# Two short terms in one product, later placement of one weight row, and 128 rows in every rounded product: a change to the opening of a one-core kernel

## The chip, the cores and the metric

One core of a Trainium2 chip runs the whole program. The metric is device time in microseconds (us) of that core. The kernel before took 1107.01 us, the median of three runs (1104.09 to 1109.41). PE is the matrix engine, PEld its weight load, DVE, ACT and POOL the vector, scalar and GpSimd engines, and SP the engine whose queue issues nearly all the DMAs.

## The reference

The reference takes `x` of 2 x 3008 x 256 float32 and does three things in a row:

```
X   = fft(fft(x, axis=1), axis=2).real           # 2 x 3008 x 256, then 6016 tokens x 256
h   = X @ w_in;   g = max(h, 0)**2;   Y = g @ w_out          # 256 -> 2048 -> 256
h   = Y @ w2_in;  P = a0 + a1*h + a2*h**2 + a3*h**3
Q   = 1 + |b0|*|h| + |b1|*h**2;   out = (P / (Q + 1e-6)) @ w2_out
```

The four weight matrices arrive as float64. The kernel turns each into a float32 on the chip and splits it into a rounded high part and a low part (`hi`, `lo`), so that a product is made of three fast products in the rounded type f32r. A product in plain f32 is made of two passes of the matrix engine, and shows as two PE instructions.

## The kernel before, in words

The Fourier transform over 3008 = 64 x 47 points is a product with 47-point tables (the "U phase"), a product along the 256 features (`f_d`, lines 488 and 489), and a 64-point product (`f_s`, lines 511 to 518). The 64 residues fold to 31 pairs of rows and two single ones. The two single ones are the first terms `x0` (line 251); the 31 others come in chunks of four rows (`X_CH`, chunks 1 to 7), then two, then one. A row has 188 terms for each feature: 128 in one slice, 60 in another. The host lays two rows beside one another as three slices of 128 partitions: 128 terms of the first row, 128 terms of the second, and a slice that holds the 60 left of the first (partitions 0 to 59) and the 60 left of the second (64 to 123). The table `c47` has zeros where the other row's terms lie. So line 255 multiplies the 128 terms and line 256 the 60 left, both for each row by itself, and for each half of the 256 features. ACT copies one half out of PSUM (line 265), and DVE adds and subtracts the two (line 272) into `U`.

Beside that, the 16 chunks W0 to W15 of the first weight matrices are loaded (lines 328 and 330) and prepared: an absolute value on ACT (335), a clamp, two bit operations and two merges on DVE (338 to 352), a sum and a difference (359), rounding on ACT (367) and the low part on DVE (372). Row 128 of `w_in` belongs to a feature of its own. It is loaded (377), prepared (381 to 395), placed by three small DMAs on rows 0, 32 and 64 of a zeroed tile `w0` of 65 rows (400), and rounded (404). Its product with `X0` is line 624 for the first two tiles of tokens and line 643 for the other ten. `X0` comes from a product with the same weight column repeated 65 times (lines 513 and 518).

The tokens go in one tile of 384 columns and eleven of 512. Each tile passes the first layer (`h1`, lines 623 to 643, and `o1`, line 669), and then the second (`h2`, line 610, and `o2`, line 669) in halves of 256 columns. Where a half's `o2` begins, one product of a row of zeros with a row of weights (line 660) clears a whole bank of PSUM.

A planner (`Queues`) sets the order: each operation has an engine, a cost in us, a place and buffers that it takes and gives, and the planner writes the operations out in the order in which its own clock starts them. An engine then runs its instructions in that order. `HOT0` and `HOT` put products on a tile of zeros (`hot_t`, line 281) ahead of and between the chunks of the U phase; `SPILL_W` says after which weight chunk `U` is written to memory for the later tiles (line 320).

Of the kernel before, what the change touches and what calls it, by code (L numbers as in the profile page):

```python
# [47 lines left out]
U_SPLIT, U_REST = 0, -7.32  # L48
HOT0, HOT = 8, (2, 11, 6, 2, 0, 0, 0, 0, 0)
DMA_LAT = 2.41  # L50
C_AT, S_AT, S_STEP = -21.12, -5.27, 3
W_AT = (-4.0, 20.0)
AB_AT = -40
W_TAGS = (("g2", "x2h", "g2", "x2l"), ("g2",))
W2_AT, W2_STEP = 6.94, 1.11
W_FIRST, SPILL_W = (0, 0, 1, 1, 2, 2, 3, 3, 4, 4), 12

# [100 lines left out]
def body(ctx: ExitStack, tc: tile.TileContext, x0, xf, w1i, w1o, w2i, w2o, a_in, b_in,  # L158
# [15 lines left out]
    ab = const.tile([128, 6], F32, name="ab")  # L174
    w0f = const.tile([65, NF, 128], F32, name="w0")
    w0 = w0f.bitcast(F32R)
    zero = const.tile([1, 128], F32R, name="zero")
    a0, a1, a2, b0 = (ab[:, i:i + 1] for i in (0, 1, 2, 4))
# [55 lines left out]
    def x_load(c):  # L234
        XT[c] = stp.tile([128, 6, 256], F32, tag="xt", name="xt", bufs=SLOTS["xt"])
        if c == 0:
            nc.sync.dma_start(out=XT[c][0:96, 0:4].rearrange("p (s h) d -> p s h d", h=2), in_=x0)
            return
        p = (S0[c] - 1) // 2
        for k in range((XN[c] + 1) // 2):  # L240
            o, a = XT[c][:, 3 * k:3 * k + 3], xf[p + k]
            if 2 * k + 2 > XN[c]:
                o, a = o[:, 0:3:2], a[:, 0:3:2]
            nc.sync.dma_start(out=o, in_=a)

    def u_mm(c, dc, tag):
        PU[c, dc] = p = ps(tag, [128, 4, 128])
        d = slice(dc * 128, (dc + 1) * 128)
        if c == 0:
            for i in range(4):  # L250
                nc.tensor.matmul(p[:, 0, 0:96], XT[c][0:96, i, d], c47_t[0:96, 3 + i], start=(i == 0), stop=(i == 3))
        else:
            for i in range(XN[c]):
                k, h = 3 * (i // 2), i % 2
                nc.tensor.matmul(p[:, i, 0:94], XT[c][:, k + h, d], c47_t[:, 0, 0:94], start=True, stop=False)
                nc.tensor.matmul(p[:, i, 0:94], XT[c][:, k + 2, d], c47_t[:, 1 + h, 0:94], start=False, stop=True)

# [27 lines left out]
    for c in range(NC):  # L285
        place = -32 + c
        n = XN[c]
        add(("x", c), "SP", 0.54 * n if c else 7.0, place, lambda c=c: x_load(c), take=("xt",), lat=X_LAT,
            after=[("wd", W_FIRST[c] - 1)] if W_FIRST[c] else [])
# [5 lines left out]
        for dc in range(2):  # L295
            add(("um", c, dc), "PE", (2 * n if c else 4) * mm4(96), place, lambda c=c, dc=dc, g=tags[dc]: u_mm(c, dc, g),
                needs=[("x", c)] + ([("hot", c)] if c and HOT[c - 1] and not dc else []), take=(tags[dc],), give=("xt",) if dc else (), lat=0.2)
# [104 lines left out]
    def w0_round():  # L402
        nc.scalar.activation(out=zero, in_=hot_t[0:1], func=ACTF.Copy)
        nc.scalar.activation(out=w0, in_=w0f, func=ACTF.Copy)
# [4 lines left out]
    add("w0p", "DVE", 1.6, -31, w0_parts, needs=["w0a"], give=("g2",), port=True)  # L409
    add("w0c", "SP", 2.4, -31, w0_place, needs=["w0p", "w0z"], give=("cw",), lat=2.5)  # L410
    add("w0", "ACT", act(2048), -20, w0_round, needs=["w0c"])
# [94 lines left out]
    def f_s(t, k, tag):  # L506
        v = FU.pop((t, k, "v"))
        f = ps(tag, [128, 512])
        FU[t, k] = p, r = f[:, 0:256].rearrange("p (c n) -> p c n", c=2), f[0:65, 256:384]
        if t + k == 0:  # L510
            nc.tensor.matmul(p[:, 0, :], v[:, 0:128], r0c, start=True, stop=True)
            nc.tensor.matmul(p[:, 1, :], v[:, 129:257], r0s, start=True, stop=True)
            nc.tensor.matmul(r, v[:, 128:129].to_broadcast([66, 65]), r0c, start=True, stop=True)
        else:
            for u in range(2):
                cols = slice(u * 64, u * 64 + 64)
                nc.tensor.matmul(p[:, :, cols], v[:, u, 0:128], rcs[:, u], start=True, stop=True)
                nc.tensor.matmul(r[:, cols], v[:, u, 128:129].to_broadcast([128, 65]), rcs[:, u, 0], start=True, stop=True)


    def f_eh(t, k, i):
        if i == 0:
            X1[t] = [sb("x1" + part, [128, 2, NMAX // 2], F32R) for part in "hl"]
            X0[t] = sb("x0", [65, NMAX // 2], F32R)
        cols = slice(i * 128, i * 128 + 128)
        p, r = FU[t, k]
        nc.scalar.activation(out=X1[t][0][:, :, cols], in_=p, func=ACTF.Copy)
        nc.scalar.activation(out=X0[t][:, cols], in_=r, func=ACTF.Copy)
# [123 lines left out]
    def mm_o(G, W, O, tag, t, j, first, gs):  # L652
        n = NW[t] if tag == "o1" else SUB[t][2]
        one = tag == "o2" and t > 0
        if j == 0:
            if one:
                o = ps("o2a", [128, NMAX])[:, :2 * n]
                O[t], OB[t] = [o[:, :n], o[:, n:]], o

                nc.tensor.matmul(o, zero, W["hi"][0][0:1, :2 * n], start=True, stop=False)  # L660
            else:
                O[t] = [ps((o1_tag(t) if tag == "o1" else tag) + part, [128, NMAX])[:, :n] for part in "ab"]
# [356 lines left out]
```

## Time and profile before

| | |
|---|---|
| Median of three runs | 1107.01 us |
| The profiled execution | 1106.53 us, its span 1104.8 us |
| PE busy | 1069.3 us, 7790 instructions |
| DVE busy | 1012.6 us |
| ACT busy | 985.7 us |
| POOL busy | 489.9 us |
| Mean granted clock of PE | 0.995 |

The span runs from the first to the last instruction; 1.7 us of the execution lie around it. A row of the timeline gives the start, the length, the engine and line, and the tiles written and read; matmuls overlap, so that the cost of one in a stream is the distance from its start to the next one's, not its length. A form such as `65*128 65x256` is 65 rows by 128 columns of weights, and 256 columns that pass through them.

### The profile page before, as it was taken

The numbers are of one execution on the slowest core, as the hardware profiler recorded it, in microseconds if no ns is written. First come the engines' busy times: TensorE is split into PE (matmuls) and PEld (weight loads), VectorE is DVE, ScalarE is ACT, GpSimd is POOL, SyncE is SP. The second block draws the span as 40 slices with busy tenths as digits, with TensorE's granted clock in tenths as the row PEclk, the third lists the DMA queues.
The fourth block names the chain that finished last, engine by engine and source line by source line (L and its number), as shares of the span: only waits on it lengthen the run. The fifth ranks groups of instructions, "written<-read, shape, count | busy, mean of one in ns | idle before, by whom it ended". The sixth has DMA issues, their size and how long they took to land.

```text
span 1104.8 us, 21504 instructions
## 1 busy us (share of the span) xinstructions
PE 1069.3 (97%) x7790; PEld 1003.3 (91%) x7790; DVE 1012.6 (92%) x1806; ACT 985.7 (89%) x2009; POOL 489.9 (44%) x373
## 2 busy tenths in 40 slices
PE   7999988999999999999999999999999999999986
PEld 7989987899999999989999999999998999999985
DVE  2799999999999999999998999999899999889997
ACT  2488887999998989899999999999999999999896
POOL 0000003545545555455545545545544555545476
PEclk9999989999999999999999999999999999999999
DMA  6753410000000000000000000000000000000000
GB/s 228 259 207 99 160 39 1 2 25 11 1 20 11 1 20 11 1 20 11 1 12 18 1 11 20 2 11 20 1 20 11 2 10 11 1 10 11 1 11 20
DMA packets 26838, 36.83 MB, mean 33 GB/s; under 512 B 2315, under 2 KB 19341, under 8 KB 26733
## 3 DMA queue, kind: packets, MB, share of 16 engines
q1 hardware_dynamic: 26589, 35.33, 9.6%
q8 instruction: 62, 1.02, 0.4%
q14 instruction: 43, 0.35, 0.1%
q10 hardware_dynamic: 144, 0.13, 0.0%
HBM read 26.65 MB, written 8.78 MB: 32 GB/s over the span
## 4 chain that ended last, share of the span: by engine, by line
PE 61%; DVE 17%; ACT 16%; issue 4%; DMA 1%; POOL 1%; SPq 0%; DVEq 0%; POOLq 0%; ACTq 0%
PE o2a L669 15%; PE p L610 12%; PE o1a L669 7%; PE o1b L669 7%; PE p L641 5%; PE o2b L610 3%; DVE g L775 2%; PE o2b L641 2%; ACT y L758 2%; DVE p L781 2%; ACT t L735 2%; ACT y L762 2%; DVE t L749 2%; ACT u L745 2%; DVE t L753 1%
## 5 line engine op out<-in xcount | busy, mean ns | idle before, releaser
L792 POOL TENSOR_TENSOR g<-t,y 128x512 fp32r<-128x512 f32 (+1 forms) x182 | 247.1, 1358 | 406.9 <-DVE t L788 312.5
L712 POOL TENSOR_TENSOR g<-g,g 128x512 fp32r<-128x512 f32 x160 | 213.1, 1332 | 189.9 <-ACT g L707 131.9
L669 PE MATMUL o2a<-g,w2hi 128*128 128x256 f32 (+1 forms) x1440 | 263.0, 283 | 5.8 <-POOL g L792 5.5
L669 PEld LDWEIGHTS o2a<-g,w2hi 128*128 128x128 f32 x1440 | 209.1, 189 | 16.6 <-POOL g L792 7.8
L775 DVE SCALAR_TENSOR_TENSOR g<-t,ab,y 128x512 fp32r<-128x512 f32 (+1 forms) x177 | 140.9, 798 | 11.1 <-ACT y L762 8.3
L669 PE MATMUL o2a<-g,w2lo 128*128 128x256 f32 (+1 forms) x720 | 144.4, 280 | 0.0
L669 PE MATMUL o1a<-g,w1hi 128*128 128x512 f32 x352 | 139.7, 397 | 1.5 <-DVE g L712 1.0
L669 PE MATMUL o1b<-g,w1hi 128*128 128x512 f32 x352 | 138.9, 395 | 0.0
L781 DVE SCALAR_TENSOR_TENSOR p<-u,g 128x512 f32<-128x512 f32 (+2 forms) x178 | 132.1, 742 | 0.7
L788 DVE SCALAR_TENSOR_TENSOR t<-t,ab,p 128x512 f32<-128x512 f32 (+2 forms) x178 | 129.0, 724 | 1.2
L741 DVE SCALAR_TENSOR_TENSOR u<-u,ab,p 128x512 f32<-128x512 f32 (+1 forms) x141 | 102.1, 724 | 26.6 <-ACT t L735 25.7
L745 ACT ACTIVATE u<-u 128x512 f32<-128x512 f32 (+2 forms) x178 | 110.0, 619 | 13.8 <-DVE u L741 13.4
L610 PE MATMUL p<-x2h,w2hi 128*128 128x256 f32 (+1 forms) x558 | 114.8, 287 | 6.6 <-DVE t L753 2.3
L762 ACT ACTIVATE y<-y 128x512 f32<-128x512 f32 (+1 forms) x185 | 115.0, 623 | 1.4
L758 ACT ACTIVATE y<-u 128x512 f32<-128x512 f32 (+1 forms) x177 | 109.3, 618 | 5.0 <-POOL g L792 2.5
L610 PE MATMUL p<-x2l,w2hi 128*128 128x256 f32 (+1 forms) x558 | 113.0, 284 | 0.0
L610 PE MATMUL p<-x2h,w2lo 128*128 128x256 f32 (+1 forms) x558 | 112.9, 284 | 0.0
L697 ACT ACTIVATE g<-g 128x512 f32<-128x512 f32 x160 | 100.7, 630 | 11.8 <-DVE g L687 11.2
L703 ACT ACTIVATE g<-g 128x512 fp32r<-128x512 f32 (+1 forms) x175 | 109.4, 625 | 2.0 <-PE o1b L669 0.5
L669 PEld LDWEIGHTS o2a<-g,w2lo 128*128 128x128 f32 x720 | 110.3, 188 | 0.0
L707 ACT ACTIVATE g<-g 128x512 f32<-128x512 f32 (+1 forms) x175 | 109.0, 624 | 1.0
L753 DVE SCALAR_TENSOR_TENSOR t<-t,ab,p 128x512 f32<-128x512 f32 (+1 forms) x143 | 103.0, 721 | 0.5
(272 smaller groups left out, 2886.8 us busy)
## 6 DMA issues: line engine op xcount, KB each, us to landing
g<-in_dram SPq DMA_DIRECT2D x48, 256.0 KB, 3.2
xt<-in_dram SPq DMA_DIRECT2D x16, 384.0 KB, 7.0
out_dram<-os SPq DMA_DIRECT2D x21, 256.0 KB, 2.1
udram<-U SPq DMA_DIRECT2D x4, 640.0 KB, 5.6
ut<-udram SPq DMA_DIRECT2D x10, 256.0 KB, 3.0
x2h<-in_dram SPq DMA_DIRECT2D x8, 256.0 KB, 5.7
x2l<-in_dram SPq DMA_DIRECT2D x8, 256.0 KB, 5.1
out_dram<-os SPq DMA_DIRECT2D x2, 192.0 KB, 1.9
```

What stands on the lines that cost most here:

```text
L610: nc.tensor.matmul(h[:, c * n:(c + 1) * n], l[:, k, :], r[:, k], start=(q == 0), stop=(q == 5))
L669: nc.tensor.matmul(O[t][e], l[:, e * 128:(e + 1) * 128], r[:, c * n:(c + 1) * n], start=(i == 0 and q == 0 and not one), stop=(i == NF - 1 ...
L703: nc.scalar.activation(out=e["gh"], in_=e["g"], func=ACTF.Square)
L712: eng.tensor_tensor(out=e["gl"], in0=e["g"], in1=f32(e["gh"]), op=ALU.subtract)
L745: nc.scalar.activation(out=w, in_=w, func=ACTF.Abs)
L753: nc.vector.scalar_tensor_tensor(out=t1, in0=t1, scalar=a1, in1=H2[t, j], op0=ALU.add, op1=ALU.mult)
L758: nc.scalar.activation(out=e["z"], in_=e["w"], func=ACTF.Abs_reciprocal_sqrt, bias=Q1)
L762: nc.scalar.activation(out=z, in_=z, func=ACTF.Square)
L775: nc.vector.scalar_tensor_tensor(out=e["gh"], in0=e["t1"], scalar=a0, in1=e["z"], op0=ALU.add, op1=ALU.mult)
L781: nc.vector.scalar_tensor_tensor(out=e["m"], in0=e["w"], scalar=Q1, in1=f32(e["gh"]), op0=ALU.add, op1=ALU.mult)
L788: nc.vector.scalar_tensor_tensor(out=e["t1"], in0=e["t1"], scalar=a0, in1=e["m"], op0=ALU.add, op1=ALU.subtract)
L792: nc.gpsimd.tensor_tensor(out=e["gl"], in0=e["t1"], in1=e["z"], op=ALU.mult)
```

## The change

The two rows' terms that are left (60 each) go through one product of 188 columns for both rows, the 128 terms of each row follow as before, and line 256 is gone. The first terms `x0` are issued by ACT's queue, ahead of its first instruction. The small tables `a` and `b` go from the head of SP's queue to a place behind weight chunk W7. The three placing DMAs of row 128 wait until chunk 6 of `x` is issued. The products on zeros between the chunks go (21 of them), and the first group has ten in place of eight. `U` is written out after W16 in place of W12. `w0`, `X0` and the zeros have 128 rows in place of 65 and 1, and so the weight column of lines 513 and 518 is repeated 128 times.

```diff
-HOT0, HOT = 8, (2, 11, 6, 2, 0, 0, 0, 0, 0)
+HOT0, HOT, W0_AFTER = 10, (0, 0, 0, 0, 0, 0, 0, 0, 0), 6
-AB_AT = -40
+AB_AT = 0
-W_FIRST, SPILL_W = (0, 0, 1, 1, 2, 2, 3, 3, 4, 4), 12
+W_FIRST, SPILL_W = (0, 0, 1, 1, 2, 2, 3, 3, 4, 4), 16
-    w0f = const.tile([65, NF, 128], F32, name="w0")
+    w0f = const.tile([128, NF, 128], F32, name="w0")
-    zero = const.tile([1, 128], F32R, name="zero")
+    zero = const.tile([128, 128], F32R, name="zero")
...
-            nc.sync.dma_start(out=XT[c][0:96, 0:4].rearrange("p (s h) d -> p s h d", h=2), in_=x0)
+            nc.scalar.dma_start(out=XT[c][0:96, 0:4].rearrange("p (s h) d -> p s h d", h=2), in_=x0)
...
-            for i in range(XN[c]):
-                k, h = 3 * (i // 2), i % 2
-                nc.tensor.matmul(p[:, i, 0:94], XT[c][:, k + h, d], c47_t[:, 0, 0:94], start=True, stop=False)
-                nc.tensor.matmul(p[:, i, 0:94], XT[c][:, k + 2, d], c47_t[:, 1 + h, 0:94], start=False, stop=True)
+            for i in range(0, XN[c], 2):
+                k, m = 3 * (i // 2), min(2, XN[c] - i)
+                nc.tensor.matmul(p[:, i:i + m, 0:94], XT[c][:, k + 2, d], c47_t[:, 1:1 + m, 0:94], start=True, stop=False)
+                for h in range(m):
+                    nc.tensor.matmul(p[:, i + h, 0:94], XT[c][:, k + h, d], c47_t[:, 0, 0:94], start=False, stop=(h == m - 1))
...
-        nc.scalar.activation(out=zero, in_=hot_t[0:1], func=ACTF.Copy)
+        nc.scalar.activation(out=zero, in_=hot_t, func=ACTF.Copy)
-    add("w0c", "SP", 2.4, -31, w0_place, needs=["w0p", "w0z"], give=("cw",), lat=2.5)
+    add("w0c", "SP", 2.4, -31, w0_place, needs=["w0p", "w0z"], give=("cw",), lat=2.5, after=[("x", W0_AFTER)])
...
-        FU[t, k] = p, r = f[:, 0:256].rearrange("p (c n) -> p c n", c=2), f[0:65, 256:384]
+        FU[t, k] = p, r = f[:, 0:256].rearrange("p (c n) -> p c n", c=2), f[:, 256:384]
-            nc.tensor.matmul(r, v[:, 128:129].to_broadcast([66, 65]), r0c, start=True, stop=True)
+            nc.tensor.matmul(r, v[:, 128:129].to_broadcast([66, 128]), r0c, start=True, stop=True)
-                nc.tensor.matmul(r[:, cols], v[:, u, 128:129].to_broadcast([128, 65]), rcs[:, u, 0], start=True, stop=True)
+                nc.tensor.matmul(r[:, cols], v[:, u, 128:129].to_broadcast([128, 128]), rcs[:, u, 0], start=True, stop=True)
-            X0[t] = sb("x0", [65, NMAX // 2], F32R)
+            X0[t] = sb("x0", [128, NMAX // 2], F32R)
-                nc.tensor.matmul(o, zero, W["hi"][0][0:1, :2 * n], start=True, stop=False)
+                nc.tensor.matmul(o, zero, W["hi"][0][:, :2 * n], start=True, stop=False)
```

The planner's costs for `x` and for the products of the U phase change with it, and with them the places of many later operations.

The head of SP's queue before; `c_t` is the table `c47`, `ab` the tables `a` and `b`, `xt` the slices of `x`, `g_137` the raw row 128, `g_169` and `x2h` raw weights, `w_73` the tile `w0`:

```order
L207 DMA c_t<-in_dram 128x672
L212 DMA ab<-in_dram 128x4
L212 DMA ab<-in_dram 128x2
L237 DMA xt<-in_dram 96x1024
L244 DMA xt<-in_dram 128x768 x2
L377 DMA g_137<-in_dram 16x256
L209 DMA cd_t<-in_dram 128x514
L209 DMA r_t<-in_dram 66x256
L328 DMA g_169<-in_dram 128x2x256
L330 DMA g_169<-in_dram 128x512
L244 DMA xt<-in_dram 128x768 x2
L400 DMA w_73<-cw 1x16x128 x3
```

The same queue after, as far as the loads of chunk 5; the placing of `w_73` (now line 402) follows only behind a weight chunk and chunk 6:

```order
L207 DMA c_t<-in_dram 128x672
L244 DMA xt<-in_dram 128x768 x2
L379 DMA g_134<-in_dram 16x256
L209 DMA cd_t<-in_dram 128x514
L209 DMA r_t<-in_dram 66x256
L330 DMA g_138<-in_dram 128x2x256
L332 DMA g_138<-in_dram 128x512
L244 DMA xt<-in_dram 128x768 x4
L330 DMA x2h<-in_dram 128x2x256
L332 DMA x2h<-in_dram 128x512
L244 DMA xt<-in_dram 128x768 x4
```

`ab` and the first `xt` left the head of the queue, and nothing that waits for another engine's work on row 128 stands ahead of the chunks of `x` any more.

PE's first rows, with what went and what came; `o1a` to `o2b` are banks of PSUM:

```order
-L281 MATMUL p_118<-hot_t 128x128 x8
+L282 MATMUL p_119<-hot_t 128x128 x10
 L251 MATMUL o1a<-c_t,xt 128x96 x4
 L251 MATMUL o1b<-c_t,xt 128x96 x4
-L281 MATMUL p_154<-hot_t 128x128 x2
-L255 MATMUL o2a<-c_t,xt 128x94
-L256 MATMUL o2a<-c_t,xt 128x94
...
+L255 MATMUL o2a<-c_t,xt 128x2x94
+L257 MATMUL o2a<-c_t,xt 128x94 x2
```

For two rows and one half of the features, four products of 94 columns became one of 188 and two of 94, and no product on zeros stands between the chunks.

PE before, where the first product of zeros with weights clears a bank (the second tile's first half of `o2`):

```order
L517 MATMUL o2b<-cd_t,v 128x2x64
L518 MATMUL o2b<-cd_t,v 65x64
L517 MATMUL o2b<-cd_t,v 128x2x64
L518 MATMUL o2b<-cd_t,v 65x64
L660 MATMUL o2a<-w2hi_1172,zero 128x512
L669 MATMUL o2a<-g_2703,w2hi_1172 128x256 x2
```

And after:

```order
L519 MATMUL p_2732<-cd_t,v 128x2x64
L520 MATMUL p_2732<-cd_t,v 128x64
L519 MATMUL p_2732<-cd_t,v 128x2x64
L520 MATMUL p_2732<-cd_t,v 128x64
L663 MATMUL o2a<-w2hi_1136,zero 128x512
L672 MATMUL o2a<-g_2598,w2hi_1136 128x256 x2
```

The sequence is the same, in the same place; line 518's output has 128 rows in place of 65.

## Rows read from the trace of the kernel before

**Rows 1.** Stretches: us; busy us (count) of PE, PEld, DVE, ACT, POOL; granted clock, DMA, GB/s.

```profile
0.00:20.00 20.00, 13.98 (x81) 13.71 (x82) 3.29 (x14) 3.02 (x7) 2.01 (x5) 1.00 0.57 181
20.00:48.00 28.00, 27.52 (x246) 27.18 (x245) 19.32 (x47) 9.99 (x22) 0.00 (x0) 1.00 0.87 303
70.00:150.00 80.00, 79.95 (x565) 76.06 (x565) 76.94 (x163) 69.06 (x146) 0.00 (x0) 1.00 0.41 132
150.00:159.00 9.00, 6.63 (x33) 5.27 (x31) 7.78 (x17) 8.91 (x20) 0.00 (x0) 1.00 0.00 1
159.00:166.00 7.00, 6.13 (x23) 6.13 (x24) 6.09 (x12) 5.17 (x13) 2.04 (x2) 0.52 0.00 0
280.00:1000.00 720.00, 716.09 (x5292) 671.10 (x5291) 675.78 (x1151) 677.38 (x1359) 369.12 (x274) 1.00 0.03 10
```

**Rows 2.** SP's queue in order of time: start us, us, engine, line, operation, count.

```profile
1.19 0.89 SPq L212 DMA_DIRECT2D ab<-in_dram  x2
...
9.69 1.34 SPq L244 DMA_DIRECT2D xt<-in_dram  x2
15.50 1.87 SPq L400 DMA_DIRECT2D w<-cw  x3
17.42 0.57 SPq L244 DMA_DIRECT2D xt<-in_dram  x1
```

**Rows 3.** Stretches of the opening: us, granted clock, DMA share, GB/s.

```profile
3.00:6.00 3.00, 1.00 0.27 45
...
14.00:18.00 4.00, 1.00 0.05 16
...
20.00:30.00 10.00, 1.00 1.00 362
```

**Rows 4.** PE in order of time, in the opening (idle before, and what ended it).

```profile
1.06 3.79 PE L281 MATMUL p<-hot_t 128*128 128x128 f32 x16 [1.06 <-DVE hot_t L276]
9.81 2.00 PE L251 MATMUL o1a<-c_t,xt 96*128 96x96 f32 x8 [4.96 <-DMA xt<-in_dram]
11.60 1.91 PE L251 MATMUL o1b<-c_t,xt 96*128 96x96 f32 x8
...
25.94 0.36 PE L255 MATMUL o1a<-c_t,xt 128*128 128x94 f32 x2
...
29.49 0.64 PE L281 MATMUL p<-hot_t 128*128 128x128 f32 x4
```

**Rows 5.** DVE in order of time, the last piece of the U phase.

```profile
47.55 0.32 DVE L272 TENSOR_TENSOR U<-g,o1b 128x94 f32<-128x94 f32 x1
```

**Rows 6.** PE in order of time, at the first product that clears a bank.

```profile
232.43 0.28 PE L518 MATMUL o2b<-cd_t,v 128*65 128x64 f32 x2
232.54 0.44 PE L517 MATMUL o2b<-cd_t,v 128*128 128x128 f32 x2
232.82 0.28 PE L518 MATMUL o2b<-cd_t,v 128*65 128x64 f32 x2
233.03 0.49 PE L660 MATMUL o2a<-w2hi,zero 1*128 1x512 f32 x1
233.45 0.51 PE L669 MATMUL o2a<-g,w2hi 128*128 128x256 f32 x2
233.79 0.39 PE L669 MATMUL o2a<-g,w2lo 128*128 128x256 f32 x2
```

**Rows 7.** Whole span, PE and PEld of line 518, then of line 660.

```profile
0.00:1105.00 1105.00, 13.09 (x92) 11.79 (x92) 1.00 0.10 33
0.00:1105.00 1105.00, 10.91 (x22) 3.98 (x22) 1.00 0.10 33
```

**Rows 8.** PE in order of time, one chunk of the first layer.

```profile
401.26 0.28 PE L641 MATMUL p<-x1l,w1hi 128*128 128x256 f32 x1
401.38 0.28 PE L643 MATMUL p<-x,w 65*128 65x256 f32 x1
401.50 0.28 PE L641 MATMUL p<-x1h,w1hi 128*128 128x256 f32 x1
401.62 0.28 PE L641 MATMUL p<-x1h,w1lo 128*128 128x256 f32 x1
401.74 0.28 PE L641 MATMUL p<-x1l,w1hi 128*128 128x256 f32 x1
```

More of the change, by code (lines that the diff above doesn't have):

```diff
@@ L287, in body @@
         n = XN[c]
-        add(("x", c), "SP", 0.54 * n if c else 7.0, place, lambda c=c: x_load(c), take=("xt",), lat=X_LAT,
+        add(("x", c), "SP" if c else "ACT", 0.54 * n if c else 0.5, place if c else -50, lambda c=c: x_load(c), take=("xt",),
+            lat=X_LAT if c > 1 else 4.0 if c else 5.0,
             after=[("wd", W_FIRST[c] - 1)] if W_FIRST[c] else [])
@@ L295, in body @@
         for dc in range(2):
-            add(("um", c, dc), "PE", (2 * n if c else 4) * mm4(96), place, lambda c=c, dc=dc, g=tags[dc]: u_mm(c, dc, g),
+            add(("um", c, dc), "PE", (0.39 * n + 0.06 * (n == 1)) if c else 0.9, place, lambda c=c, dc=dc, g=tags[dc]: u_mm(c, dc, g),
                 needs=[("x", c)] + ([("hot", c)] if c and HOT[c - 1] and not dc else []), take=(tags[dc],), give=("xt",) if dc else (), lat=0.2)
```

## The prediction, made before the changed kernel ran

> **What bounds the kernel now.** I read the stretches first [rows 1]. From 280 to 1000 us PE is busy for 716.09 of 720 us, while DVE has 675.78 and ACT 677.38: the long middle is bound by PE, with some 40 us to spare on the next engines. From 70 to 150 us PE has 79.95 of 80 and DVE 76.94: both are full there, because DVE still prepares weights. In the first 20 us DVE has 3.29 and in the next 28 us 19.32: the opening is the one place in which neither engine has its work, and whatever brings that work forward should reach the end whole, as long as the full stretch behind it only slides.
>
> Next I read who makes the opening wait. PE's first real product starts at 9.81 us after 4.96 us idle, ended by the DMA of the first terms [rows 4]. That DMA stands behind the two tiny loads of `a` and `b`, issued from 1.19 us [rows 2]; from 3 to 6 us the DMA engines move 45 GB/s, against 362 from 20 to 30 us [rows 3]. So it was not bytes that held the first terms back but the many small pieces of `a` and `b` ahead of them. A second hole follows: SP issues two loads of `x` at 9.69 us, and then nothing until 15.50, where it places row 128 after waiting for DVE's work on it; the next load of `x` goes out at 17.42 [rows 2]. From 14 to 18 us the DMA engines move 16 GB/s [rows 3]. The U phase ends with DVE's last piece, at 47.55 + 0.32 = 47.87 us [rows 5].
>
> **The change part by part.**
>
> *The opening: the end of the U phase.* I work out when each of the three resources could finish it, and take the latest.
> - DMA. `c47` (0.344 MB) and the first terms (0.393 MB) now lie at the head, on two queues: 0.737 MB at 362 GB/s [rows 3] is 2.0 us, from about 2 us on (`c47` is issued at under 1 us, its packets follow by an estimated 1 us), so about 4.2. All bytes until the last of `x` (table, first terms, 15.5 pairs of rows of 0.786 MB for two, row 128, two tables, four weight chunks of 0.524 MB) are 9.3 MB, 25.7 us at that rate: about 28 us.
> - PE. Ten products on zeros are 20 passes; 16 took 3.79 us [rows 4], so 4.7, from 1.06 to 5.8: the first terms are there. Their 16 passes cost (11.60 - 9.81) / 8 = 0.224 us each [rows 4], 3.6 us, until 9.4. These passes are at the lower clock level: in the fast part a pass of line 255 costs (29.49 - 25.94) / 32 = 0.111 us [rows 4], half as much, though the row of the stretch writes 1.00 for both [rows 1]; I read it that no level is on record before the first change. Two rows and one half now take two passes of 188 columns and four of 94. A pass of 188 columns is not in the trace: at least 0.111 (if the weight load alone set it), at most 0.222 (in proportion to 94); a fast pass of 128 columns is 3.79 / 16 / 2 = 0.118, which gives 188/128 x 0.118 = 0.17. I take 0.16, near that row. A group is 2 x 0.16 + 4 x 0.111 = 0.76 us, against 8 x 0.111 = 0.89 before. 15 pairs with two halves are 30 groups, 22.9 us, and the single row 0.9: 23.8 us, until 33.2. The 21 products on zeros between the chunks (42 passes, some 5 us) are not in it any more. DVE's last pieces follow by about 1 us: 34.2.
> - DVE. It did 3.29 + 19.32 = 22.6 us of work until 48 us [rows 1], and its list to the same point is the same. It can start when row 128 has landed, about 7 us: 30 us, if it never waits.
>
> The three lie within 6 us, and an order that mixes weights and rows will make them wait for one another a little: I put the end at 36, so 12 us sooner. Bounds: 15 us (PE's list, first terms at the fast level) and 6 us (only the DMA hole of 4 us and half of what the first terms gain). Everything behind it (weights, `f_d`, the first `h1`) depends on the same DVE list and on weight loads that also come sooner, so the full stretch from 70 us slides. -12.
>
> The Trainium skill (Trainium Kernel Development and Optimization, Key Constraints) says that DMAs of the several queues share the same 16 engines and that a second issuer saves only issue time. By that, ACT's queue by itself would give the first terms the 0.89 us of SP's two `ab` issues and no more; the trace has no second queue in the opening to test it on. It doesn't touch the sum, which rests on `ab` being gone from the head.
>
> *The clearing product.* With one row, line 660 disturbs three steps [rows 6]: the two passes before it take 233.03 - 232.82 = 0.21 us where the same two took 0.11 at 232.43; it takes 0.42 where 512 columns cost two steps of 0.115 to 0.12 [rows 8], 0.23; and the two products behind it take 0.34, where two such steps are 0.23. Together 0.10 + 0.19 + 0.11 = 0.40 us, 22 times [rows 7]: 8.8. Full 128-row products don't show this. Some of the 22 stand where PE waits anyway, and PE's gain is at times taken by DVE or ACT at 94%: I take -7.0. Bounds -8.8 and 0.
>
> *The repeated column.* Line 518 steps by (232.54 - 232.43) / 2 = 0.055 us with 65 columns of weights [rows 6]. With 128 I expect the 0.111 that every f32 pass with 128 columns of weights has [rows 4]: +0.056, 92 times [rows 7], +5.2. Bounds 0 (as if hidden) and 5.2; nearly all of it lies in the full stream: +4.7.
>
> The Trainium skill (TensorE: Matmul & The Clock Gate, LDWEIGHTS) puts the time of a weight load on its columns, and says that the number of rows doesn't matter, 32 x 128 as 128 x 128. Line 518's step agrees with the first half; the second half would leave line 660 as it is, and its 0.42 us for one row speaks against it. It has a rival of its own below.
>
> *Row 128's product.* Lines 641 behind line 643 step by 0.12, the ones ahead of it by 0.11 to 0.12 [rows 8]. If 65 rows are the cause, it is up to 0.01 for two or three steps in each of 160 chunks: bounds -4 and 0. The row is too coarse to lean on: -1.
>
> *The rest.* The absolute value of `b` and two register loads on ACT come from an idle place to a busy one, behind a DMA that ACT must wait for: 0 to 1.5, +0.5. `U`'s writing comes later, but still well ahead of the third tile's use, at no cost. Zeroing and rounding 128 rows in place of 65 have the same columns: 0. The planner's new order moves PE's blocks by a few places all through the run: +-3, 0 in the sum.
>
> Sum: -12 - 7.0 + 4.7 - 1 + 0.5 = -14.8 on the profiled execution's 1106.5 (1104.8 of span and 1.7 around it): 1091.7. The median of the runs is 0.5 above that execution: I say 1092.
>
> **The rivals.**
> - *The opening gives half.* PE's products, DVE's list and the loads are each nearly as long, so one late weight chunk (or ACT, waiting for row 128's placing, which is now in the thick of the U phase) stalls the others. For it: the three bounds above lie close. Against it: the holes that go, at 3 to 6 and 14 to 18 us, are plain. -6 - 3 (zeros less what the column costs, the rest): about 1098.
> - *Rows cost nothing.* Line 660's 0.40 us belongs to a lone product between accumulation groups and stays; the columns still cost. Against it: its 512 columns take nearly twice the step of other products. -12 + 4.7 + 0.5: 1099.7. The Trainium skill's sentence on weight loads (TensorE: Matmul & The Clock Gate, LDWEIGHTS) would have it so.
> - *Slower: PE at the lower clock through the U phase.* The 42 passes on zeros filled the waits between chunks. If PE waits for `x` and its clock stays at or falls to 1.2 GHz, the passes double: 23.8 becomes 47.6, and the U phase ends at 9.4 + 47.6 + 1 = 58, 10 us later than before, so 1106.5 + 10 - 3 = 1113. It decides once more than half of the chunks (some 12 us of fast PE work) run at the lower level. For it: after 2.4 us of idle PE from 150 to 159 us, the clock's mean is 0.52 from 159 to 166 [rows 1]. Against it: a chunk of PE work (4 groups, 3.06 us) is as long as its bytes (0.786 MB and half a weight chunk at 362 GB/s, 2.9 us), and PE starts with two chunks of lead.
> - *The stretch from 150 to 166 us* (PE idle 2.4 us, then 7 us at half the clock) comes out worse in the new order, and takes 5: 1097.
>
> **How the numbers follow.** My forecast 0.70 (by itself 1085 to 1100), the half opening 0.12, rows that cost nothing 0.09, the slow clock 0.05, the later stretch 0.04. Reaching to the first two rivals and a little under the forecast: 1083 to 1102. What this kernel's measurement can tell from no change is about 0.5%, 5.5 us: faster means under 1101.5. Of the forecast 0.96 lies there, of the half opening 0.85, of the third 0.65, of the last 0.6: 0.67 + 0.10 + 0.06 + 0.02 = 0.85. Slower: 0.05. The same: 0.10.
>
> **What would show it.** Line 251 starting near 6 us; lines 255 and 257 without long idle time, at steps of 0.16 and 0.11, ending near 33; DVE's last piece of U near 36; the first `h1` (line 623's successor) as much sooner as that. The clearing product at a step of 0.23, with 0.11 ahead of it; line 518's successor at 0.11. The prediction is wrong if U ends after 42 us, if the step at the clearing product is still 0.42, or if the clock's mean in the first 40 us shows the lower level beyond 12 us.

## The result and the profile after

The changed kernel takes 1088.55 us (median of 4 runs, 1088.07 to 1088.86), beside 1107.70 of the kernel before on the same chip (4 runs, 1104.09 to 1109.41): a ratio of 0.9831, with a 95% interval of 0.9812 to 0.9850. The forecast was 1092 in a range of 1083 to 1102. The profiled execution took 1088.24, its span is 1086.3; against the profiled execution of before it is 18.3 shorter. Of the five runs of one kernel below (a pair in four products) two took 1117.6 us, in a slower state of the chip, and its median is that of the other three.

The stretches of the changed kernel, with the columns of [rows 1]:

```profile
0.00:20.00 20.00, 18.62 (x128) 18.09 (x129) 10.48 (x31) 5.57 (x12) 2.01 (x5) 1.00 0.95 333
20.00:34.00 14.00, 12.71 (x101) 12.37 (x99) 11.66 (x31) 7.30 (x15) 0.00 (x0) 1.00 0.99 341
56.00:136.00 80.00, 78.75 (x561) 75.11 (x561) 76.01 (x162) 69.25 (x146) 0.00 (x0) 1.00 0.48 156
...
145.40:148.80 3.40, 3.40 (x11) 2.79 (x10) 2.93 (x6) 3.09 (x9) 0.00 (x0) 0.50 0.00 0
260.00:980.00 720.00, 713.65 (x5301) 673.01 (x5300) 675.27 (x1153) 679.87 (x1363) 370.30 (x274) 1.00 0.03 10
```

DVE has 10.48 us of work in the first 20, where it had 3.29. The U phase now ends inside the second row, near 34 us, not 48. In the long middle PE has 713.65 of 720 (716.09 before): 2.4 us less busy in as long a stretch, while the stretch also holds more of the work. The 3.4 us at the clock of 0.50 stand where 6.8 us at about half stood before. Three kernels below (zeros of one row, `ab` at the head, pairs in four products) show no such stretch there, so the 1.7 us that this saves can't be put down to the change.

SP's queue, to be laid beside [rows 2]:

```profile
1.19 0.89 SPq L244 DMA_DIRECT2D xt<-in_dram  x2
...
14.74 0.95 SPq L244 DMA_DIRECT2D xt<-in_dram  x2
16.40 4.07 SPq L402 DMA_DIRECT2D w<-cw  x3
20.87 0.34 SPq L244 DMA_DIRECT2D xt<-in_dram  x1
```

Loads of `x` now stand where the two tiny loads of `ab` stood, and SP issues loads until 15.7. It still stands at the placing of row 128, for 4.07 us, but the loads that are under way by then carry the DMA engines across. The same stretches as [rows 3], for the changed kernel:

```profile
3.00:6.00 3.00, 1.00 1.02 354
14.00:18.00 4.00, 1.00 1.05 402
20.00:30.00 10.00, 1.00 0.99 336
```

45 GB/s became 354, and 16 became 402: both holes are gone. PE in the opening, beside [rows 4], and DVE's last piece, beside [rows 5]:

```profile
5.84 1.10 PE L251 MATMUL o1a<-c_t,xt 96*128 96x96 f32 x8 [0.19 <-DMA c_t<-in_dram]
6.78 1.06 PE L251 MATMUL o1b<-c_t,xt 96*128 96x96 f32 x8
7.67 0.51 PE L255 MATMUL o2a<-c_t,xt 128*128 128x188 f32 x2
8.02 0.58 PE L257 MATMUL o2a<-c_t,xt 128*128 128x94 f32 x4
8.44 0.51 PE L255 MATMUL o2a<-c_t,xt 128*128 128x188 f32 x2
...
31.92 0.39 PE L257 MATMUL o1b<-c_t,xt 128*128 128x94 f32 x2
33.60 0.44 PE L490 MATMUL p<-cd_t,U 128*66 128x130 f32 x2 [1.29 <-DVE U L273]
```

```profile
33.60 0.32 DVE L273 TENSOR_TENSOR U<-g,o1b 128x94 f32<-128x94 f32 x1
```

What ended the wait ahead of line 251 is now the table (0.19 us) and not the first terms (4.96). A group of a pair is 8.44 - 7.67 = 0.77 us, as forecast (0.76). PE runs from 5.84 to about 32.3 with only two short waits for `x` (0.3 and 0.15 us, near 11 and 12 us); the 1.29 us behind it are the wait for DVE's last pieces. So PE's list is the length of the opening, and DVE follows it by a little.

PE at the first clearing product (beside [rows 6]), and one more of the 22 behind a chunk of the first layer (beside [rows 8]):

```profile
217.21 0.33 PE L520 MATMUL p<-cd_t,v 128*128 128x64 f32 x2
217.38 0.44 PE L519 MATMUL p<-cd_t,v 128*128 128x128 f32 x2
217.66 0.33 PE L520 MATMUL p<-cd_t,v 128*128 128x64 f32 x2
217.80 0.47 PE L663 MATMUL o2a<-w2hi,zero 128*128 128x512 f32 x1
218.12 0.39 PE L672 MATMUL o2a<-g,w2hi 128*128 128x256 f32 x2
218.34 0.39 PE L672 MATMUL o2a<-g,w2lo 128*128 128x256 f32 x2
...
710.88 0.28 PE L646 MATMUL p<-x,w 128*128 128x256 f32 x1
710.99 0.28 PE L644 MATMUL p<-x1h,w1hi 128*128 128x256 f32 x1
...
711.22 0.28 PE L644 MATMUL p<-x1l,w1hi 128*128 128x256 f32 x1
711.33 0.39 PE L663 MATMUL o2a<-w2hi,zero 128*128 128x512 f32 x1
711.55 0.40 PE L672 MATMUL o2a<-g,w2hi 128*128 128x256 f32 x2
```

The product on 128 rows of zeros takes 0.32 and 0.22 us to the next start (0.22 to 0.34 over all 22, where one row took 0.42 or 0.43 each time), with 0.11 ahead of it at 711 and 0.22 for the two products behind it at 218. The repeated column (line 520) takes 217.38 - 217.21 = 0.17 for two passes, not 0.11: of a pair, the first pass still steps by 0.058 and only the second by 0.111. Over the whole span (beside [rows 7]), line 520 and then line 663:

```profile
0.00:1086.30 1086.30, 15.33 (x92) 13.94 (x92) 1.00 0.10 34
0.00:1086.30 1086.30, 9.30 (x22) 4.13 (x22) 1.00 0.10 34
```

### The profile page after: what moved, and what is told of

Its sections match the earlier page's. It is cut to its first block, busy times and chain, and to the rows that moved or that the text cites. A ratio compares the mean times of both kernels' runs of the same rounds, so it can differ in the third digit from the quotient of the medians.

```text
span 1086.3 us, 21308 instructions
## 1 busy us (share of the span) xinstructions
PE 1053.5 (97%) x7692; PEld 992.0 (91%) x7692; DVE 1009.5 (93%) x1806; ACT 987.5 (91%) x2009; POOL 491.7 (45%) x373
## 4 chain that ended last, share of the span: by engine, by line
PE 51%; ACT 28%; DVE 13%; issue 6%; DMA 2%; POOL 1%; SPq 0%; ACTq 0%; POOLq 0%; DVEq 0%
PE o2a L672 13%; PE p L613 9%; PE o1a L672 6%; PE o1b L672 6%; PE p L644 4%; ACT y L761 4%; PE o2b L613 3%; ACT t L738 3%; ACT g L700 3%; ACT g L706 3%; ACT u L748 3%; ACT y L765 3%; ACT u L733 2%; DVE p L784 2%; ACT g L710 2%
## 5 line engine op out<-in xcount | busy, mean ns | idle before, releaser
L795 POOL TENSOR_TENSOR g<-t,y 128x512 fp32r<-128x512 f32 (+1 forms) x182 | 249.9, 1373 | 423.2 <-DVE t L791 194.8
L672 PEld LDWEIGHTS o2a<-g,w2hi 128*128 128x128 f32 x1440 | 212.0, 189 | 13.9 <-POOL g L795 9.4
L778 DVE SCALAR_TENSOR_TENSOR g<-t,ab,y 128x512 fp32r<-128x512 f32 (+1 forms) x177 | 137.4, 778 | 13.1 <-ACT y L765 12.0
L613 PE MATMUL p<-x2h,w2hi 128*128 128x256 f32 (+1 forms) x534 | 109.5, 286 | 8.4 <-DVE x1h L789 3.9
L744 DVE SCALAR_TENSOR_TENSOR u<-u,ab,p 128x512 f32<-128x512 f32 (+1 forms) x134 | 97.1, 725 | 19.9 <-ACT t L738 18.9
L613 PE MATMUL p<-x2h,w2lo 128*128 128x256 f32 (+1 forms) x534 | 107.2, 282 | 0.0
L613 PE MATMUL p<-x2l,w2hi 128*128 128x256 f32 (+1 forms) x534 | 107.2, 282 | 0.0
L690 DVE TENSOR_TENSOR g<-p,bc 128x256 f32<-128x256 f32 x238 | 96.6, 417 | 5.5 <-ACT bc L680 3.3
```

The costliest lines, as they stand in the source:

```text
L613: nc.tensor.matmul(h[:, c * n:(c + 1) * n], l[:, k, :], r[:, k], start=(q == 0), stop=(q == 5))
L672: nc.tensor.matmul(O[t][e], l[:, e * 128:(e + 1) * 128], r[:, c * n:(c + 1) * n], start=(i == 0 and q == 0 and not one), stop=(i == NF - 1 ...
L778: nc.vector.scalar_tensor_tensor(out=e["gh"], in0=e["t1"], scalar=a0, in1=e["z"], op0=ALU.add, op1=ALU.mult)
L795: nc.gpsimd.tensor_tensor(out=e["gl"], in0=e["t1"], in1=e["z"], op=ALU.mult)
```

## The experiments

Two times of each profiled execution sort everything that follows: when the first product of the first transform starts (line 490 here, line 488 before), and how long it is from there to the end of the last instruction that computes (the span ends 2.7 us later in each). The first tells the opening, the second all the rest.

```
kernel                          median us  ratio to before      first transform  from there to the end
before                          1107.70    -                    47.55            1054.46
changed                         1088.55    0.9831 +-0.0019      33.60            1050.01
rows alone                      1101.18    0.9943 +-0.0019      46.27            1049.17
opening alone                   1092.88    0.9858 +-0.0019      33.95            1054.29
clearing product alone          1101.39    0.9952 +-0.0019      46.32            1049.68
changed, zeros of one row       1092.47    0.9857 +-0.0021      34.05            1055.82
changed, column 65 times        1089.32    0.9833 +-0.0021      37.01            1048.35
changed, ab at the head         1091.33    0.9863 +-0.0022      35.83            1050.96
changed, row 128 placed early   1092.37    0.9874 +-0.0020      38.59            1049.41
changed, pairs in four products 1089.01    0.9855 +-0.0029      36.56            1047.25
changed, zeros between chunks   1095.67    0.9903 +-0.0020      42.19            1050.94
changed, first terms on SP      1088.87    0.9828 +-0.0021      34.76            1050.51
changed, old order from 150 us  1094.77    0.9884 +-0.0020      33.46            1056.62
the same with column 65 times   1091.69    0.9855 +-0.0021      33.53            1054.04
```

Each ratio is to runs of before on the same chip, whose median moved between 1105.43 and 1108.58; so the ratios are compared, and differences of 2 us are not told apart by medians alone.

### Rows alone, opening alone

The first question was where the two halves of the gain lie, and whether the planner's new order costs something in the middle: between the second and the twentieth clearing product the changed kernel took 744.99 us and the kernel before 746.36, where 18 steps at 0.39 had promised 7 less. Theory A put that on the new order, theory B on waits. The kernel before with 128 rows everywhere:

```
-    w0f = const.tile([65, NF, 128], F32, name="w0")
-    zero = const.tile([1, 128], F32R, name="zero")
+    w0f = const.tile([128, NF, 128], F32, name="w0")
+    zero = const.tile([128, 128], F32R, name="zero")
...
-                nc.tensor.matmul(o, zero, W["hi"][0][0:1, :2 * n], start=True, stop=False)
+                nc.tensor.matmul(o, zero, W["hi"][0][:, :2 * n], start=True, stop=False)
```

The repeated column and its operands go from 65 to 128 likewise.

> The kernel before with 128 rows in the zeros, w0 and X0 (and so the column repeated 128 times), nothing else; the order on every engine is that of before. From the steps after, PE should save 22 x 0.39 = 8.6 us at the clearing products and 160 x 0.015 = 2.4 us behind row 128's product, and lose 46 x 0.055 = 2.5 us at the repeated column: 8.5 us of PE time. Theory A (the new order of the middle costs about 4 us, and the rows' gain arrives whole): 1107.7 - 8.5 = 1099. Theory B (the order is neutral, and about half of PE's gain in the middle is lost to waits for DVE, ACT and POOL): 1107.7 - 4 = 1103.5. The rival of the prediction by which rows cost nothing: no faster than before.

And the changed kernel with 65 rows and one row, as before:

```
-    w0f = const.tile([128, NF, 128], F32, name="w0")
-    zero = const.tile([128, 128], F32R, name="zero")
+    w0f = const.tile([65, NF, 128], F32, name="w0")
+    zero = const.tile([1, 128], F32R, name="zero")
...
```

> The changed kernel with 65 and 1 rows as before (w0, X0, zeros, column), its opening and its order kept. Theory A: the opening's 14 us less the 4 us that the order costs, 1107.7 - 10 = 1097.5. Theory B: the opening's 14 us arrive whole, 1107.7 - 14 = 1093.5, about 5 us above the changed kernel. In both the first f_d starts near 33.6 us.

Rows alone gave 7.4 us, opening alone 15.7; the first lies between the theories, the second is B's number. The table says more than the medians: with the opening alone the first transform starts 13.60 us sooner, and what follows takes 1054.29 beside 1054.46. The opening arrives whole at the end, and the new order costs next to nothing over all (before has 3.4 us more at the lower clock behind the opening, so a cost of 1.7 us could be hidden). With rows alone the second time falls by 5.29, on top of the new opening by 4.28. The rest of the 7.4 is not the rows': with the same instructions ahead of them, the first terms start at 8.26 us in rows alone and at 8.46 in the clearing product alone, where they start at 9.81 in the profiled execution of before. So the old opening's first transform starts anywhere from 46.3 to 47.6, and the new opening is worth 12.7 to 14 us.

### Zeros of one row, and the clearing product alone

```
-    zero = const.tile([128, 128], F32R, name="zero")
+    zero = const.tile([1, 128], F32R, name="zero")
...
-                nc.tensor.matmul(o, zero, W["hi"][0][:, :2 * n], start=True, stop=False)
+                nc.tensor.matmul(o, zero, W["hi"][0][0:1, :2 * n], start=True, stop=False)
```

> The changed kernel with one row in the clearing product again, all else and the order kept. Its step should be 0.43 again with 0.09 more on each side, 8.6 us of PE time. Theory A: 1088.5 + 8.6 = 1097. Theory B: about half, 1088.5 + 4 = 1092.5.

3.9 us slower by the medians, as B had it, but 2.9 by the ratios, at the edge of the noise. The trace is clearer: every step is 0.42 or 0.43 again, the steps at the 18 products between the second and the twentieth and at their two neighbours grow by 6.3 us together, and that stretch by 3.6 (744.99 to 748.58). The reverse edit in the kernel before, and nothing else:

> The kernel before with the clearing product alone on 128 rows of zeros; row 128's product and the repeated column stay at 65. Theory Half column (the column costs on every second pass only, 46 x 0.055 = 2.5 us, and row 128's product gives about as much back, 160 x 0.015 = 2.4): the clearing product alone gives what all rows together gave, -7 to -8, ratio 0.9930 to 0.9938. Rival Full column (the prediction's terms: column +4.7, row 128's product -1): the clearing product alone gives -10 to -11, ratio 0.990 to 0.991.

It gave 1101.39 beside 1107.03, 5.6 us: less than either theory, and by the second time 4.78. Its order is that of the kernel before, so [rows 6] has the same place:

```profile
231.42 0.44 PE L517 MATMUL o2b<-cd_t,v 128*128 128x128 f32 x2
231.70 0.28 PE L518 MATMUL o2b<-cd_t,v 128*65 128x64 f32 x2
231.78 0.48 PE L660 MATMUL o2a<-w2hi,zero 128*128 128x512 f32 x1
232.10 0.40 PE L669 MATMUL o2a<-g,w2hi 128*128 128x256 f32 x2
232.33 0.39 PE L669 MATMUL o2a<-g,w2lo 128*128 128x256 f32 x2
```

From the two passes ahead to the second product behind it is 232.33 - 231.70 = 0.63 us, where it was 0.97. Summed over the 18 products between the second and the twentieth, these three steps fell by 1.20 + 3.19 + 1.90 = 6.3 us. The stretch itself fell by 4.0 (746.36 to 742.39): stalls longer than 0.3 us grew by 1.0, and the other 1.3 is spread over the steps of other lines. So the rows do what was said on PE, and about a third of it does not arrive. That the engines beside PE take it fits the longer stalls; which of them, instruction by instruction, stays open.

### The column 65 times again

```
-            X0[t] = sb("x0", [128, NMAX // 2], F32R)
+            X0[t] = x0z[:, t % 2]
...
-        nc.scalar.activation(out=X0[t][:, cols], in_=r, func=ACTF.Copy)
+        nc.scalar.activation(out=X0[t][0:65, cols], in_=r, func=ACTF.Copy)
```

The column is repeated 65 times again; `x0z` holds two operands of 128 rows, zeroed once by GpSimd in the opening.

> The changed kernel with the column repeated 65 times; X0 keeps 128 rows, of which the last 63 are zeroed once at the start by POOL (four copies, in the idle opening). It takes back the step behind line 518's successor, 0.112 to 0.057, 46 times: 2.5 us of PE time. Theory A: 1088.5 - 2.5 = 1086. Theory B: 1088.5 - 1.2 = 1087.3. Slower than 1089 would say that the column's cost was hidden.

1089.32, no gain that can be told; the second time fell by 1.66. Two things came with it. In the opening, where GpSimd's zeroing now stands, the table landed later and PE, after 1.58 us idle, fell to the lower clock:

```profile
6.59 1.10 PE L252 MATMUL o1a<-c_t,xt 96*128 96x96 f32 x8 [1.58 <-DMA c_t<-in_dram]
7.52 1.88 PE L252 MATMUL o1b<-c_t,xt 96*128 96x96 f32 x8
```

The second eight passes take twice the first; the first transform is 3.4 us late. That the zeroing is the cause is not shown: the table is nearly as late (line 251 at 6.45) in the run with row 128 early, which zeroes nothing more. And row 128's product, though its operands have 128 rows here too, still steps by 0.1185 and 0.120 (mean of 138 chunks behind 280 us), as with 65 rows (0.120, 0.1215), not by 0.115 as in the changed kernel. What gave the changed kernel these steps is therefore not the number of rows alone; the operand also lies in another buffer here. What the cause is stays open.

### The opening, part by part

Five runs undid one part each; the two products more at the head and the later writing of `U` were not undone by themselves. First the two loads of `ab` at the head (`AB_AT = -40`):

> The changed kernel with the two tiny loads of a and b at the head of SP's queue again (first terms still on ScalarE's queue). Theory Head (the first terms were late because of these loads' many small pieces on shared DMA engines): line 251 starts near 9.5 us in place of 5.84, f_d follows 3 to 3.6 us later, and the time is 1091.5 to 1092. Rival Queue (it was the place behind them in one queue that made the first terms late; from a second queue they pass): line 251 starts within 1 us of 5.84, the time is 1088.5 to 1089.5.

PE and the DMA engines in that run (the second fence as [rows 3], with all engines' busy time):

```profile
5.88 1.25 PE L251 MATMUL o1a<-c_t,xt 96*128 96x96 f32 x8 [0.19 <-DMA c_t<-in_dram]
...
8.51 0.59 PE L255 MATMUL o2a<-c_t,xt 128*128 128x188 f32 x2 [0.49 <-DMA xt<-in_dram]
...
13.63 0.59 PE L255 MATMUL p<-c_t,xt 128*128 128x188 f32 x2 [1.60 <-DMA xt<-in_dram]
```

```profile
4.70:6.20 1.50, 1.31 (x7) 1.04 (x6) 0.00 (x0) 0.00 (x0) 0.00 (x0) 1.00 0.07 8
```

On the mechanism the rival Queue is right: line 251 starts at 5.88, because ScalarE's queue passes the small pieces. The time is near Head's (ratio 0.9863; 2.8 us, at the edge of the noise; 2.23 at the first transform): what stands behind `ab` in SP's queue, the loads of `x`, is held instead. The engines move 8 GB/s for 1.5 us, and PE waits 0.49 + 1.60. The small pieces stop their own queue, not the 16 engines. The Trainium skill (Trainium Kernel Development and Optimization, Key Constraints) lets a second queue save only the time of an issue; here it saved the first terms the whole wait behind `ab` (line 251 at 5.88, where it started at 8.26 to 9.81 behind `ab` in one queue).

Where no such load is ahead, the two queues differ little. First terms back on SP's queue, behind the table:

```
-            nc.scalar.dma_start(out=XT[c][0:96, 0:4].rearrange("p (s h) d -> p s h d", h=2), in_=x0)
+            nc.sync.dma_start(out=XT[c][0:96, 0:4].rearrange("p (s h) d -> p s h d", h=2), in_=x0)
```

> The changed kernel with the first terms on SP's queue, behind the first table and ahead of the rest; order of all else the same. Theory Shared engines (a second queue saves only the time of an issue): line 251 starts 0 to 0.6 us later, the time is 1088.5 to 1089.5. Rival Clock (the longer wait behind the products on zeros keeps PE at the lower level until 14 us, as in the run with 65 columns): f_d 3 to 4 us later, 1091.5 to 1092.5.

1088.87: no difference in the medians, and line 251 starts at 5.76, as Shared engines had it. The loads of `x` now stand one place later in the queue, though: PE waits 1.0 us for one of them, and the first transform starts 1.16 us later. The medians are too coarse to show so much.

Row 128 placed early (`after=[("x", W0_AFTER)]` taken from line 412):

> The changed kernel with row 128 placed as early as the planner likes, not behind the loads of x. Theory Hole (SP stands at the placing until DVE's parts are there, and the loads of x behind it come late): PE waits 2 to 4 us for x between 10 and 25 us, f_d follows 2 to 3 us later, the time is 1090.5 to 1091.5. Rival Lead (SP waits anyway: in the changed kernel it stands 4.07 us at the same placing, only later, and the loads ahead of it carry PE across): within 0.5 us of the changed kernel, 1088.5.

3.8 us slower, so it is not Lead, and the hole is where Hole had it. The DMA engines in it:

```profile
11.40:13.80 2.40, 2.18 (x15) 1.97 (x15) 2.28 (x5) 0.43 (x3) 0.00 (x0) 1.00 0.30 47
```

ACT's copies of banks `o2a` and `o1a`, and the wait of PE:

```profile
11.32 0.47 ACT L266 ACTIVATE g<-o2a 128x376 f32<-128x376 f32 x1
...
20.99 0.47 ACT L266 ACTIVATE g<-o1a 128x376 f32<-128x376 f32 x1
```

```profile
21.47 0.56 PE L255 MATMUL o2a<-c_t,xt 128*128 128x188 f32 x2 [2.50 <-ACT g L266]
```

The row puts PE's wait down to ACT's copy that ends at 21.46. That can't be it: this copy empties `o1a`, and the product writes `o2a`, which was empty at 11.79. What the product reads is the seventh load of `x`, and SP issues it only behind the placing; SP's queue, and the size and time to landing of that one load (the DMA view from 14.4 to 14.7 us):

```profile
14.56 2.10 SPq L244 DMA_DIRECT2D xt<-in_dram  x4
```

```profile
xt<-in_dram SPq DMA_DIRECT2D x1, 384.0 KB, 6.8
```

So it landed at some 21.3 us, when PE's queue stopped waiting for its semaphore; in the changed kernel, where it was issued at 9.64, it landed at 16.33. PE waited 2.50 us for `x`, inside Hole's 2 to 4. That the first transform comes 5.0 us later, and not 2 to 3, has two more causes in this execution: the table landed 0.6 us later, and after the wait PE's clock fell to 0.50 from 22.79 to 26.20, which costs 1.7.

The old four products of 94 columns for a pair, in a run of their own; and in another the 21 products on zeros between the chunks (`HOT = (2, 11, 6, 2, ...)`):

```
...
+                nc.tensor.matmul(p[:, i, 0:94], XT[c][:, k + h, d], c47_t[:, 0, 0:94], start=True, stop=False)
+                nc.tensor.matmul(p[:, i, 0:94], XT[c][:, k + 2, d], c47_t[:, 1 + h, 0:94], start=False, stop=True)
```

> The changed kernel with four products of 94 columns for a pair of rows (8 passes of 0.111 us) in place of one of 188 and two of 94 (0.765 us); order as in the changed kernel. PE list theory (PE was without a gap from 6.78 to 32.2 us, so its list is the opening's length): 30 x 0.125 = 3.7 us on PE, 1.3 of them in the wait for DVE that stands behind; f_d 2.4 us later, 1091. Rival DVE list (DVE's weights and pieces set the end, PE only follows): f_d at most 0.7 us later, 1088.5 to 1089.2.

> The changed kernel with the 21 products on zeros between the first chunks again (42 passes). PE list theory: 42 x 0.118 = 5.0 us more on PE, 1.3 in the wait behind; f_d 3.7 us later, 1092.3. Rival (they stand where PE would wait or save a fall of the clock): within 0.7 us, 1088 to 1089.2.

With four products the first transform starts 2.96 us later (2.4 forecast by the PE list): PE's list is the opening's length. The median is only 0.5 us up, inside the rival's range, and by the ratio 2.7 us, neither of them clear of noise; in this profiled execution no stretch at the lower clock is on record, where the changed kernel's has two of 3.4 us. So it is the first transform that decides for the PE list, not the time. With the zeros the first transform starts 8.6 us later, more than the 3.7: the products themselves took 5.2, and PE stayed at the lower clock until 13.94 us, not 5.47. The late rise is not shown to be theirs: the first of them starts at 12.55, and until then PE has the same products as in the changed kernel (of chunk 1 the other half first). Its first terms:

```profile
6.10 1.99 PE L251 MATMUL o1a<-c_t,xt 96*128 96x96 f32 x8 [0.41 <-DMA c_t<-in_dram]
7.88 1.92 PE L251 MATMUL o1b<-c_t,xt 96*128 96x96 f32 x8
```

They cost 3.49 us in place of 1.83. The idle time ahead is 0.41 us, against 0.19 in the changed kernel.

### The old order from the second layer's first output on

The two kernels that keep the order of before and have 128 rows, rows alone and zeros between chunks, take 741.40 and 741.83 us between the second and the twentieth clearing product, the changed kernel 744.99. If that is the price of the order, the old order behind the new opening should give 3.5 us. The planner was run twice, with the old costs (`was`) and with the new (`now`), and its lists were joined at the first product of the second layer's output, near 153 us (the expectation calls it the first clearing product, but that one comes at 217.80):

```
...
+    cut = was.index(CUT)
+    head, mine = set(was[:cut]), set(now)
+    for fn in queues.run([k for k in now if k in head] + [k for k in was[cut:] if k in mine])[0]:
```

> The changed kernel with only the planner's order replaced: as in the changed kernel up to the first clearing product (some 150 us), from there on the order of the kernel before. Same instructions. Theory Order (the planner's new order costs PE about 3.5 us between the second and the twentieth clearing product, by small waits): that stretch falls from 744.99 to 741.4 to 741.9 us, the value of the two kernels that had the old order with 128 rows, and the time to 1084.5 to 1086. Rival Full (with less PE work, DVE and ACT are late here and there in any order, and the two kernels differed in something else): the stretch stays at 744 to 745.5, the time at 1088 to 1089.

> The order of the run before the last two (opening as changed, then the order of the kernel before), with the column repeated 65 times and row 128's operand kept at 128 rows, its other rows zeroed once by GpSimd. Theory Every second pass (the 128-wide column costs PE 46 x 0.055 us): the stretch between the second and the twentieth clearing product falls by 1.5 to 2.5 us, and the time is 1082.5 to 1084 if the opening's clock rises as early as in the changed kernel, 3 us more if it rises at 14 us. Rival Hidden (those steps are covered by DVE and ACT in this order): the stretch moves by less than 0.7 us.

The stretch fell to 741.93, just as Order said, and the kernel became 6 us slower, 1094.77. Both theories fail. Up to the join it is level with the changed kernel. From 160 to 180 us, the joined order and then the changed kernel:

```profile
160.00:180.00 20.00, 13.49 (x71) 11.50 (x72) 16.94 (x32) 12.66 (x31) 6.81 (x6) 1.00 0.00 0
```

```profile
160.00:180.00 20.00, 19.34 (x112) 17.20 (x111) 19.24 (x40) 18.65 (x42) 9.77 (x8) 1.00 0.01 1
```

PE lost 5.9 us there. The two orders do the same work in another sequence, so a clearing product of the same number does not stand behind the same amount of other work: between the first `h1` of the third tile and the second clearing product PE has 644 products in the changed kernel and 654 in rows alone. From the first `h1` of the third tile to the second clearing product the changed kernel needs 100.90 us and rows alone 104.76: the new order is 3.9 us ahead there, and gives 3.6 back in the stretch that I had taken for its cost. From that first `h1` to the end it is 927.14 and 927.47. The changed kernel has 10 products fewer left there (1.1 us), so the order costs 1 us or so, and not 3.5; the window had measured a shift. The loss at the join says nothing on the old order as a whole. With the column 65 times the stretch fell by another 2.0 (739.93), as Every second pass had it, and the median by 3.1; the time of 1082.5 to 1084 had built on the joined order being the faster one, and missed by 8.

No version beats the changed kernel by more than the measurement can tell.

## Why the prediction was right, point by point

- **The bound.** Right: holes in the opening, PE in the middle. What the opening gains reaches the end whole: 13.95 us at the first transform, 18.4 at the end, and most of the rest is the rows' (4.3).
- **The opening, -12.** Right in its parts, too small by 2 (by 0.7 against the old opening of the two other traces): U's last piece starts at 33.60, not near 36. What held the first terms back was not the small pieces of `ab` as such, as the prediction has it, but their place behind them in one queue. The first terms ran at the fast level (1.83 us, not 3.6), PE's list ended near 32.3, not 33.2, and DVE and PE hardly waited for one another. Each part undone costs time at the first transform: `ab` 2.2, the placing 5.0 (2.3 of it clock and a late table), the pairs 3.0, the zeros 8.6 (some 3.1 of it clock). Their sum is 18.8, and 13.4 without the clock and the late table. The first terms' own queue by itself is worth 1.2 there, and nothing that the medians show.
- **The clearing product, -7.0.** The step was right (0.40 forecast; 0.35 in the sum over 18, 0.34 at [rows 6]'s place). What arrives is 4.8 to 5.6 alone and 2.9 to 3.9 in the new order: the term was too large by 2 or more. The reason given for a loss, PE's gain taken by other engines at 94%, weighs more than was said (2.3 of 6.3 us, not 1.8 of 8.8), and is not traced to an instruction.
- **The repeated column, +4.7.** The step that failed. I gave every pass 0.056 more; only the second of each pair pays (0.056 to 0.111), the first stays at 0.058: 46 x 0.055 = 2.5, of which 1.7 and 2.6 show in the second times of the two runs with 65 columns. I had taken the step of f32 passes on another line for both.
- **Row 128's product, -1.** These steps gave 2.2 between the second and the twentieth clearing product (lines 641 and 643 of before, 1.47 + 0.77 over the steps without a stall, in rows alone). The size is off, inside its bounds; that 65 rows are the cause is not shown, and the run with the column 65 times speaks against it.
- **The rest and the order, +0.5 and +-3.** Opening alone: -0.2 behind the first transform, with 3.4 us less at the lower clock. Right.
- **The rivals.** The opening gave more than half. Rows that cost nothing are refuted by rows alone and by the clearing product alone; one row of operand took 0.42 us to the next start, 128 rows 0.22 to 0.34. The Trainium skill's sentence (TensorE: Matmul & The Clock Gate, LDWEIGHTS), by which the number of rows does not matter, is on the weight load alone. There the trace agrees: 22 loads of one row took 3.98 us, of 128 rows 4.13; so the prediction and its rival took from it more than it says when they applied it to the product's step. The slow clock did not come in the changed kernel's U phase, but it came in three neighbours: from 7.56 to 14.39 with the column 65 times, until 13.94 with the zeros, at a cost of some 3 us each, and from 22.79 to 26.20 with row 128 early, at 1.7. The later stretch came 1.6 us worse (23.30 us from the first `h2` product to the first `h1` of the third tile, 21.74 before), though its clock was low for half as long; it was not 5.

The errors partly cancel: opening -2, column -2.2, row 128 -1.2, the rest -0.7, clearing +2.2, together -3.9, where the result lies 3.5 us below the forecast. That it lies so near is in part luck: the clearing product and the column were each wrong by some 2 us, in opposite directions.

## What to carry to other kernels

Find the last of the resources that a start-up phase needs (loads, PE's list, the next engine's list), and look in each queue for what stands ahead of the first useful load: a load of tiny pieces, or a transfer that waits for another engine, holds everything behind it in that queue. A gain in a start-up phase arrives whole when the full stretch behind it only slides. When two orders are compared, measure from one common state to the end: a window between instructions of the same name measures how the order is shifted as well.

## What the runs showed of the hardware that was not expected

- A product of one operand row and 512 columns takes 0.42 us to the next start and lengthens the step ahead of it (0.21 for 0.12) and the one behind (0.22 for 0.12); with 128 rows of zeros it takes 0.22 to 0.34, and these two steps are 0.12. Its weight load is nearly as long in both (3.98 and 4.13 us for 22).
- A repeated column of 128 in place of 65 lengthens only the second of two passes (0.056 to 0.111 us).
- Two loads of 3 KB in all, in small pieces, leave the engines at 8 GB/s for 1.5 us while another queue's 0.39 MB is not held up.
- With the new opening PE's clock rose between 3.96 and 6.56 us in ten of the eleven kernels, during the products on zeros or the first terms, and in one only at 13.94, though PE had the same products until 12.55. In one of the ten it fell from 7.56 to 14.39, after PE had stood idle for 1.58 us, and in another from 22.79 to 26.20, after 2.50 us. What decides between these cases is not shown. The two long stretches cost some 3 us each (3.4 us later at the first transform, 0.75 of it the late table; 8.6 later, 5.2 of it the products), the short one 1.7.
